# Score products of two pairs of heads in one visit, with the second pair in the banks that the products with V used

## The chip, the cores and the metric

The program runs on one core of one Trainium2 chip. Its time is the time of one execution on the device in microseconds; the runs before the change gave 1420.03, 1419.76 and 1416.32 us, median 1419.76 us. TensorE (PE in the profile) does the matrix products and writes them to PSUM, 8 banks of 512 float32 values in each of 128 partitions; VectorE (DVE), ScalarE (ACT) and GpSimd (POOL) do the rest, DVE and ACT alone reading PSUM here; SyncE (SP) issues nearly all DMAs.

## What is computed

The reference is an attention whose heads are mixed before and after the softmax, followed by two feed-forward blocks:

```python
scores = scale * np.matmul(q, k.transpose(0, 1, 3, 2))      # batch 4, heads 12, seq 448, dim 64
scores = np.einsum('bhij,hg->bgij', scores, w_pre)
attn = np.exp(scores - np.max(scores, axis=-1, keepdims=True))
attn = attn / (np.sum(attn, axis=-1, keepdims=True) + 1e-09)
attn = np.einsum('bhij,hg->bgij', attn, w_post)
x = np.matmul(attn, v)                                       # to (1792, 768)
h = x @ w_in;  x = (np.maximum(h, 0) ** 2) @ w_out           # 768 -> 2048 -> 768
h = x @ w_in2; x = (h * np.clip(h + 3, 0, 6) / 6) @ w_out2
```

## The kernel before

The four batches go in two groups of two. Each group is one attention stage and then one stage of both feed-forward blocks; the attention of the second group is opened (its first score chunk, its first tiles) behind the last units of the first group's feed-forward stage. On the trace the first attention stage ends at about 245 us, the second runs from about 722 to 947 us.

**The attention stage.** The 448 rows of a batch are cut into four chunks, c, of 110, 110, 110 and 118 rows, so a group has chunks 0 to 7. For each chunk the scores of the 12 heads are written to a tile `s(c)` in SBUF (two such tiles, in turn). A DMA then gathers tiles `t` of 10 rows by 12 heads, 120 partitions by 448 columns, 11 or 12 for a chunk and 90 for a group. The loop runs over these tiles, one in a slot i (`slot`, which follows the list `ORDER`). The steps look ahead: slot i fetches tile i+6 (`LOOK`), mixes tile i+3 with `w_pre` on PE (`premix`, tile `ps_m`, two PSUM banks in turn), takes its row maximum on DVE (`top`), the exponential of tile i+2 on ACT (`soft`, tile `p`), the reciprocal of the sums of tile i+1 on DVE (`guard`, `invert`), scales the mixing matrix with it on POOL (`scale`, tile `w2s`), and mixes tile i with it on PE (`postmix`, tile `ps_o`, two banks in turn); `keep` copies tile i-1 out of PSUM on DVE. `premix` and `postmix` are float32 products, which the trace shows as two matmuls for each one written.

**Work put into slots.** `plan` puts what belongs to other chunks into slots. The scores of a chunk, `score(c, k)`, go by pairs of heads k = 0 to 5. A pair lies in the two halves of the 128 partitions, so that its two matmuls work on 64 rows each and start together on PE; each pair takes three such products (high part with high part, low with high, high with low; fp32r). They are written to `bs`, one tile of two banks, of which there is one; a copy takes both banks to `s(c)`, on DVE for k = 2 and 5 and on ACT for the others. The list `when` has a slot for each k: for chunk c of 2 and over 0, 1, 3, 4 (or 5), 6 and 7 (or 8) slots after a start four slots ahead of chunk c-1; for chunk 1 of the second group the slots 0, 0, 1, 2, 3, 4. Chunk 1 of the first group uses unsplit float32 products (`score_first`) in slots 1, 2 and 3. In a slot, the scores stand on PE between `premix` and `postmix`.

The products with V of a finished chunk, `values(c, v)` for v = 0 and 1, are 24 written matmuls each, on 112 rows by 64 columns of the array; they stood in slot `f0 + 2`, f0 being the first slot of the next chunk, and wrote to `ps_x`, two banks in turn of the tag `bx`; DVE copies them to `xr`. V of the next batch is fetched one slot behind.

**The feed-forward stage.** Its units are `hidden` and `project`. `project` adds up in six accumulators, three output blocks d for each of the two batches e: d = 0 in the tag `bo`, d = 1 in the tag `bx`, d = 2 in the two banks of `bs`. In the last of eight units they are finished batch by batch (`finish`): for the first block by ACT (`yh`, L584) and DVE (`yl`, L585), for the second by a copy of ACT (L593). Within one engine everything runs in program order.

Of the kernel before, what the change touches and what calls it, by code (L numbers as in the profile page):

```python
# [7 lines left out]
F32 = mybir.dt.float32  # L8
# [3 lines left out]
AF = mybir.ActivationFunctionType  # L12
# [14 lines left out]
EARLY = 6  # L27
IDLE = 2
# [30 lines left out]
def attention_mlp_kernel(ctx: ExitStack, tc, qT, kT, v, w_pre, w_post, mask, w1_in, w1_out, w2_in, w2_out, outT):  # L59
    nc = tc.nc  # L60
    B, _, _, S = kT.shape
# [3 lines left out]
    P = 128  # L65
# [11 lines left out]
    DB = KC // DG  # L77
# [4 lines left out]
    ps = ctx.enter_context(tc.tile_pool(name="ps", bufs=2, space=PSUM))  # L82
    dr = ctx.enter_context(tc.tile_pool(name="dr", bufs=1, space=bass.MemoryType.DRAM))

    def bank(tag, name):
        return ps.tile([128, 512], F32, tag=tag, name=name)
# [12 lines left out]
    def load_constants():  # L99
        nc.sync.dma_start(out=mk, in_=mask)  # L100
        nc.sync.dma_start(out=wa, in_=w_pre)
        nc.sync.dma_start(out=wb, in_=w_post)
# [12 lines left out]
    class Attention:  # L115
# [60 lines left out]

        def score(self, c, k):
            n = CH[self.chunks[c][1]][1]
            if c < len(self.q_raw):
                for e in range(2):  # L180
                    self.score_first(bs[:n, e, :S], c, 2 * k + e)
            else:

                qh, ql = (x[:, k % (GB // 2), :n] for x in self.live["qq", c, 2 * k // GB])
                kh, kl = self.khl[:, 0, k, :], self.khl[:, 1, k, :]
                out = [bs[:n, e, :S] if self.ap else bank("bm", f"ps_s{self.gi}_{c}_{2 * k + e}")[:n, :S]
                       for e in range(2)]
                for m, (q, kk) in enumerate(((qh, kh), (ql, kh), (qh, kl))):
                    for e in range(2):
                        own = slice(e * D, (e + 1) * D)  # L190
                        nc.tensor.matmul(out[e], lhsT=q[own], rhs=kk[own], start=(m == 0), stop=(m == 2))  # L191
                if not self.ap:
                    for e in range(2):
                        nc.scalar.activation(self.s(c)[:n, 2 * k + e, :], out[e], AF.Copy)
            if self.ap and k % 3 == 2:
                nc.vector.tensor_copy(self.s(c)[:n, 2 * k:2 * k + 2, :], bs[:n, :, :S])
            elif self.ap:
                nc.scalar.activation(self.s(c)[:n, 2 * k:2 * k + 2, :], bs[:n, :, :S], AF.Copy)

        def s(self, c):  # L200
            if c not in self.ss:
# [83 lines left out]
        def values(self, c, v):  # L285
            b, ci = self.chunks[c]
            r0, n, _, _ = CH[ci]
            xo = bank("bx", f"ps_x{self.gi}_{c}_{v}")
            for k in range(PAIRS):
                for q in range(JC):  # L290
                    for e in range(2):
                        g = 2 * (v * PAIRS + k) + e
                        nc.tensor.matmul(  # L293
                            xo[e * D:(e + 1) * D, k * n:(k + 1) * n], lhsT=self.v[:, q, g, :],
                            rhs=self.aa[c][:, q, g, :n], start=(q == 0), stop=(q == JC - 1))
            if self.xr is None:
                self.xr = sh.tile([P, KC, T], F32, tag="xr", name=f"xr{self.gi}")
            c0 = (b % NB) * S + r0
            dst = self.xr[:, v * PAIRS:(v + 1) * PAIRS, c0:c0 + n]
            src = xo[:, :PAIRS * n].rearrange("p (k i) -> p k i", i=n)  # L300
            nc.vector.tensor_copy(dst, src)
# [7 lines left out]
        def first_opening(self):  # L309

            b, nk = self.batches[0], H // 2
            ns = [CH[ci][1] for ci in range(RAW)]
            raw = sh.tile([2 * D, nk * (S + sum(ns))], F32, tag="xr", name="first")
            self.k_raw = kr = raw[:, :nk * S].rearrange("p (k j) -> p k j", j=S)
            at = nk * S
            for n in ns:
                self.q_raw.append(raw[:, at:at + nk * n].rearrange("p (k r) -> p k r", r=n))
                at += nk * n
            idle = sh.tile([P, S], F32, tag="w0", name="idle", bufs=2)
            nc.gpsimd.memset(idle, 0.0)  # L320

            def load_q(c):
                r0, n = CH[c][:2]
                src = qT[b, :, r0 * nk:(r0 + n) * nk].rearrange("p (k r) -> p k r", k=nk)
                nc.sync.dma_start(out=self.q_raw[c], in_=src)

            for k in range(0, nk, 2):
                nc.sync.dma_start(out=kr[:, k:k + 2, :], in_=kT[b, k:k + 2].rearrange("k p j -> p k j"))
                if k == 0:
                    load_q(0)  # L330

            p = bank("bx", "ps_idle")
            for k in range(IDLE):
                nc.tensor.matmul(p[:, :S], lhsT=idle[:, :P], rhs=idle, start=(k == 0), stop=(k == IDLE - 1))
            load_constants()
            for c in range(1, RAW):
                load_q(c)
            for j in range(H + EARLY):
                c, h = j // H, j % H
                n = CH[c][1]  # L340
                p = bank(("bm", "bo")[j % 2], f"ps_s{self.gi}_{c}_{h}")
                self.score_first(p[:n, :S], c, h)
                if j % 2 == 0:
                    nc.scalar.activation(self.s(c)[:n, h, :], p[:n, :S], AF.Copy)
                else:
                    nc.vector.tensor_copy(self.s(c)[:n, h, :], p[:n, :S])
                if j == GB:
                    make_constants()
# [20 lines left out]
        def plan(self):  # L369

            def put(slot, fn, *args):
                self.at.setdefault(slot, []).append((fn, args))

            nch = len(self.chunks)
            for c in range(1, nch):
                f0, ns = self.first[c - 1], self.first[c] - self.first[c - 1]
                if c == 1:

                    at, when = f0, [f0 + k * 2 * (ns - LOOK) // H for k in range(H // 2)]
                else:  # L380

                    at = f0 - LOOK + 2
                    when = [at + k * 2 * (ns - 2) // H for k in range(H // 2)]
                if c < len(self.q_raw):
                    for k in range(EARLY // 2, H // 2):
                        put(k - EARLY // 2 + 1, self.score, c, k)
                    for k in range(H // 2):
                        put(4 + k * 3 // 2, self.part_first, k)
                    continue
                for k in range(H // GB):  # L390
                    put(when[k * GB // 2] - 5, self.fetch_q, c, k)
                    put(when[k * GB // 2] - 2, self.split_q, c, k)
                for k in range(H // 2):
                    put(when[k], self.score, c, k)
                b, ci = self.chunks[c]
                if ci == len(CH) - 1 and b != self.batches[-1]:
                    for k in range(H // 2):
                        put(at + 2 * k, self.fetch_k, b + 1, k)
                        put(at + 2 * k + 1, self.split_k, b + 1, k)
            for c in range(nch - 1):  # L400
                f0, ns = self.first[c + 1], self.first[c + 2] - self.first[c + 1]
                b, ci = self.chunks[c]
                for v in range(NV):
                    at = f0 + 2
                    put(at, self.values, c, v)
                    if ci == len(CH) - 1:
                        put(at + 1, self.fetch_v, b + 1, v)
            for v in range(NV):
                put(v, self.fetch_v, self.batches[0], v)
# [47 lines left out]
    class Mlps:  # L457
# [146 lines left out]
        def run(self, mp, behind):  # L604

            rest = None
            for n, (kind, which, m, _) in enumerate(self.units):
# [14 lines left out]
                if kind == "h":  # L622
                    if m == 0:
                        nm = f"{self.gi}_{which}"
                        self.gh, self.gl = {}, {}
                        gx = sh.tile([P, KC, T], F32R, tag="xr", name=f"gx{nm}")
                        for fc in range(NF):
                            for e in range(NB):
                                for part, of in (("h", self.gh), ("l", self.gl)):
# [4 lines left out]
                                    tag, bufs = SHARED.get((part, fc, e), (f"g{part}{fc}_{e}", 1))  # L634
# [11 lines left out]
                if u == 0:  # L646
                    acc = {}
                    for e in range(NB):
                        for d in range(DB):
                            nm = f"ps_a{self.gi}_{which}_{dg}_{d}_{e}"  # L650
                            if d < DB - 1:
                                acc[d, e] = bank(("bo", "bx")[d], nm)
                            else:
                                acc[d, e] = bank("bm", nm) if alone else bs[:, e, :]
                if m == 0 and which == 0:
# [10 lines left out]
                    behind[n - (len(self.units) - 1 - len(behind))]()  # L666

    bs = ps.tile([P, 2, 512], F32, tag="bs", name="bs", bufs=1)
    groups = B // NB
    with tc.manual_schedule():  # L670
        nc.vector.memset(half, 0.5)
# [70 lines left out]
```

## Time and profile before

| what | value |
| --- | --- |
| runs, median of 3 (lowest to highest) | 1419.76 us (1416.32 to 1420.03) |
| profiled execution, span from first to last instruction | 1417.4 us |
| PE busy | 1402.9 us (99%) |
| DVE, ACT, POOL busy | 669.0, 549.3, 384.7 us |
| bytes moved by DMA | 162.68 MB, mean 115 GB/s |
| lines of the chain that hold score products in `bs` and `ps_s` (L191) | 4%, under 1% |

For the profiled execution no time beside its span is given, so what lies around the span is not shown; the span lies within the three runs. A matmul's row gives its start well and its end by a model, so times on PE are best read from start to start. Idle time of an engine other than PE costs nothing by itself.

### The profile page before, as it was taken

Reading aid. Unit: us, or ns where it says so; the run is one execution under the profiler, and the core shown is the slowest. Engines: PE = TensorE matmul, PEld = TensorE weight load, DVE = VectorE, ACT = ScalarE, POOL = GpSimd, SP = SyncE. Lnnn points to the kernel's source line nnn. Section 1 sums busy time; section 2 is a strip of 40 time slices with the busy share of each in tenths; the row PEclk is TensorE's granted clock in tenths of the full one; section 3 lists DMA queues with packets and bytes.
Section 4 is the critical chain, followed back from the end, with each engine's and each line's share of the span. In section 5 each row is a group of like instructions: output and inputs, shape, how many; then the busy total and the mean of one; then the engine's idle time right before and its main releaser. Section 6 shows DMA issues by size and latency. Waiting matters only on the chain.

```text
span 1417.4 us, 22145 instructions
## 1 busy us (share of the span) xinstructions
PE 1402.9 (99%) x8500; PEld 1191.6 (84%) x8500; DVE 669.0 (47%) x1297; ACT 549.3 (39%) x1025; POOL 384.7 (27%) x431
## 2 busy tenths in 40 slices
PE   8999999999999999999999999999999999999998
PEld 4676778899989999988966677789999999999998
DVE  4776677877665688755536667751110102111000
ACT  3554344555332355534234534444341214443121
POOL 0222122433100133300012212145552223554221
PEclk9999999999999999999999999999999999999999
DMA  5453434555555455566544434321111111211121
GB/s 165 113 142 96 123 100 126 172 165 165 167 167 167 138 164 168 167 198 197 172 119 127 131 93 124 103 79 56 56 57 56 49 53 56 56 56 56 56 91 44
DMA packets 68367, 162.68 MB, mean 115 GB/s; under 512 B 6821, under 2 KB 43429, under 8 KB 68261
## 3 DMA queue, kind: packets, MB, share of 16 engines
q1 hardware_dynamic: 64805, 155.75, 37.5%
q10 hardware_dynamic: 3456, 5.51, 1.0%
q8 instruction: 67, 1.10, 0.3%
q14 instruction: 39, 0.32, 0.1%
HBM read 92.03 MB, written 30.67 MB: 87 GB/s over the span
## 4 chain that ended last, share of the span: by engine, by line
PE 96%; DVE 2%; DMA 1%; ACT 1%; issue 0%; SPq 0%; POOL 0%; DVEq 0%; ACTq 0%
PE ps_h L561 32%; PE ps_a L575 23%; PE ps_o L266 11%; PE ps_m L218 10%; PE bs L575 9%; PE ps_x L293 5%; PE bs L191 4%; DMA t<-s 1%; PE ps_s L306 1%; PE ps_s L191 0%; DMA first<-in_dram 0%; DVE arena L501 0%; DVE wl L519 0%; DVE yl L585 0%; DVE arena L504 0%
## 5 line engine op out<-in xcount | busy, mean ns | idle before, releaser
L266 PEld LDWEIGHTS ps_o<-w2s,p 120*112 120x112 f32 (+1 forms) x1440 | 168.3, 178 | 66.4 <-issue 40.8
L517 ACT ACTIVATE wh<-arena 128x768 fp32r<-128x768 f32 x128 | 107.4, 839 | 294.3 <-PE bs L575 247.2
L575 PE MATMUL ps_a<-gh,wh 128*128 128x448 f32 x544 | 199.7, 367 | 0.0
L575 PE MATMUL ps_a<-gh,wl 128*128 128x448 f32 x544 | 198.1, 364 | 0.0
L235 ACT ACTIVATE p<-ps_m,mx 120x448 f32<-120x448 f32 x180 | 113.9, 633 | 199.1 <-PE ps_o L266 149.3
L266 PE MATMUL ps_o<-w2s,p 120*112 120x120 f32 (+1 forms) x1440 | 186.0, 273 | 1.0 <-POOL w2s L255 1.0
L519 POOL TENSOR_TENSOR wl<-arena,wh 128x768 fp32r<-128x768 f32 x64 | 118.2, 1848 | 236.4 <-ACT wh L517 233.2
L218 PE MATMUL ps_m<-t,w1f 120*120 120x448 f32 x360 | 169.9, 555 | 3.7 <-DMA t<-s 3.7
L553 POOL TENSOR_TENSOR gl<-g,gh 128x448 fp32r<-128x448 f32 x80 | 98.7, 1234 | 227.1 <-ACT gh L552 179.0
L255 POOL TENSOR_SCALAR w2s<-w2f,rz 120x120 f32<-120x120 f32 x180 | 66.1, 367 | 346.4 <-DVE rz L247 315.5
L561 PE MATMUL ps_h<-xh,wh 128*128 128x448 f32 x384 | 140.6, 366 | 0.0
L561 PE MATMUL ps_h<-xh,wl 128*128 128x448 f32 x384 | 140.3, 365 | 0.1
L561 PE MATMUL ps_h<-yh,wh 128*128 128x448 f32 x384 | 140.3, 365 | 0.0
L561 PE MATMUL ps_h<-yh,wl 128*128 128x448 f32 x384 | 140.2, 365 | 0.0
L561 PE MATMUL ps_h<-xl,wh 128*128 128x448 f32 x384 | 139.6, 364 | 0.1
L561 PE MATMUL ps_h<-yl,wh 128*128 128x448 f32 x384 | 139.4, 363 | 0.0
L281 DVE COPY a<-ps_o 112x480 f32<-112x480 f32 (+1 forms) x176 | 114.8, 652 | 46.6 <-PE ps_o L266 38.2
L575 PE MATMUL ps_a<-gl,wh 128*128 128x448 f32 x340 | 124.7, 367 | 0.0
L227 DVE TENSOR_REDUCE mx<-ps_m 120x1 f32<-120x448 f32 x180 | 111.2, 618 | 22.5 <-PE ps_m L218 19.8
L519 DVE TENSOR_TENSOR wl<-arena,wh 128x768 fp32r<-128x768 f32 x64 | 62.7, 980 | 104.8 <-ACT wh L517 103.9
L575 PEld LDWEIGHTS ps_a<-gh,wh 128*128 128x128 f32 x544 | 102.1, 188 | 10.4 <-issue 2.5
L575 PEld LDWEIGHTS ps_a<-gh,wl 128*128 128x128 f32 x544 | 102.0, 188 | 9.4 <-issue 0.6
(83 smaller groups left out, 2264.1 us busy)
## 6 DMA issues: line engine op xcount, KB each, us to landing
arena<-in_dram SPq DMA_DIRECT2D x64, 768.0 KB
t<-s SPq DMA_DIRECT2D x176, 210.0 KB
keep<-arena SPq DMA_DIRECT2D x64, 384.0 KB
arena<-keep SPq DMA_DIRECT2D x64, 384.0 KB
v<-in_dram SPq DMA_DIRECT2D x8, 672.0 KB
outT_dram<-ot ACTq DMA_DIRECT2D x24, 224.0 KB
kr<-in_dram SPq DMA_DIRECT2D x18, 224.0 KB
qr<-in_dram SPq DMA_DIRECT2D x30, 110.0 KB
```

What stands on the lines that cost most here:

```text
L218: nc.tensor.matmul(m[:rows, :S], lhsT=w1f.rearrange("p i g -> p (i g)")[:rows, :rows], rhs=self.live.pop(("t", i))[:rows], start=True, sto ...
L227: nc.vector.reduce_max(mx[:rows], m[:rows, :S], axis=AX.X, negate=True)
L235: nc.scalar.activation(pt[:rows], m[:rows, :S], AF.Exp, bias=mx[:rows], accum_out=z[:rows])
L255: nc.gpsimd.tensor_scalar(w2s[:rows, :G * ni].rearrange("p (g i) -> p g i", g=G), w2f[:rows, :, :ni], rz[:rows], 1.0, op0=ALU.mult, op1=AL ...
L266: nc.tensor.matmul(o[:JP, q * G * ni:(q + 1) * G * ni], lhsT=pt[:rows, q * JP:(q + 1) * JP], rhs=w2s[:rows, :G * ni], start=True, stop=True)
L281: nc.vector.tensor_copy(dst, src)
L293: nc.tensor.matmul(xo[e * D:(e + 1) * D, k * n:(k + 1) * n], lhsT=self.v[:, q, g, :], rhs=self.aa[c][:, q, g, :n], start=(q == 0), stop=(q ...
L517: nc.scalar.activation(wh, self.wr(n), AF.Copy)
L519: eng.tensor_tensor(out=wl, in0=self.wr(n), in1=f(wh), op=ALU.subtract)
L553: nc.gpsimd.tensor_tensor(out=gl, in0=g, in1=f(gh), op=ALU.subtract)
L561: nc.tensor.matmul(hp[:, :S], lhsT=lw[:, c * P:(c + 1) * P], rhs=rw[:, c, cols], start=(k == 0), stop=(k == 3 * KC - 1))
L575: nc.tensor.matmul(acc[d, e][:, :S], lhsT=lw[:, wc], rhs=rw[fc, e], start=(fc == 0 and k == 0), stop=(fc == NF - 1 and k == 2))
```

## The change

Pairs with odd k are written to a second tile of two banks, `bx`, which now exists once, as `bs` does; the pair k+1 is put into the slot of pair k for even k, so two pairs follow each other in one visit of PE to the scores. `values` writes to the first bank of `bx` for v = 0 and to the second bank of `bs` for v = 1, and stands two slots later. In the feed-forward stage the block d = 1 adds up in the two banks of `bx`.

```diff
         def score(self, c, k):
             n = CH[self.chunks[c][1]][1]
+            two = (bs, bx)[k % 2]
             if c < len(self.q_raw):
                 for e in range(2):
-                    self.score_first(bs[:n, e, :S], c, 2 * k + e)
+                    self.score_first(two[:n, e, :S], c, 2 * k + e)
...
-                out = [bs[:n, e, :S] if self.ap else bank("bm", f"ps_s{self.gi}_{c}_{2 * k + e}")[:n, :S]
+                out = [two[:n, e, :S] if self.ap else bank("bm", f"ps_s{self.gi}_{c}_{2 * k + e}")[:n, :S]
...
             if self.ap and k % 3 == 2:
-                nc.vector.tensor_copy(self.s(c)[:n, 2 * k:2 * k + 2, :], bs[:n, :, :S])
+                nc.vector.tensor_copy(self.s(c)[:n, 2 * k:2 * k + 2, :], two[:n, :, :S])
             elif self.ap:
-                nc.scalar.activation(self.s(c)[:n, 2 * k:2 * k + 2, :], bs[:n, :, :S], AF.Copy)
+                nc.scalar.activation(self.s(c)[:n, 2 * k:2 * k + 2, :], two[:n, :, :S], AF.Copy)
...
         def values(self, c, v):
...
-            xo = bank("bx", f"ps_x{self.gi}_{c}_{v}")
+            xo = (bx, bs)[v % 2][:, v % 2, :]
...
                     for k in range(EARLY // 2, H // 2):
-                        put(k - EARLY // 2 + 1, self.score, c, k)
+                        put(1 if k == EARLY // 2 else 2, self.score, c, k)
...
                 for k in range(H // 2):
-                    put(when[k], self.score, c, k)
+                    put(when[k // 2 * 2], self.score, c, k)
...
                 for v in range(NV):
-                    at = f0 + 2
+                    at = f0 + 4
                     put(at, self.values, c, v)
...
-                            if d < DB - 1:
-                                acc[d, e] = bank(("bo", "bx")[d], nm)
+                            if d == 0:
+                                acc[d, e] = bank("bo", nm)
+                            elif d == 1:
+                                acc[d, e] = bx[:, e, :]
...
     bs = ps.tile([P, 2, 512], F32, tag="bs", name="bs", bufs=1)
+    bx = ps.tile([P, 2, 512], F32, tag="bx", name="bx", bufs=1)
```

PE in a steady stretch, first group, slots 18 to 20 (`ps_m` is a premix, `ps_o` a postmix, `qh`, `ql` and `khl` the parts of q and k). Before:

```order
L191 MATMUL bs<-khl_300,qh_3_0_670 118x448 x2
L191 MATMUL bs<-khl_300,ql_3_0_671 118x448 x2
L191 MATMUL bs<-khl_300,qh_3_0_670 118x448 x2
L266 MATMUL ps_o_18_719<-w2s_18_683,p_18_656 112x120 x4
L218 MATMUL ps_m_22_737<-t_22_648,w1f 120x448
L191 MATMUL bs<-khl_300,qh_3_0_670 118x448 x2
L191 MATMUL bs<-khl_300,ql_3_0_671 118x448 x2
L191 MATMUL bs<-khl_300,qh_3_0_670 118x448 x2
L266 MATMUL ps_o_19_748<-w2s_19_705,p_19_680 112x120 x4
```

And with the change:

```order
L192 MATMUL bs<-khl_300,qh_3_0_668 118x448 x2
L192 MATMUL bs<-khl_300,ql_3_0_669 118x448 x2
L192 MATMUL bs<-khl_300,qh_3_0_668 118x448 x2
L192 MATMUL bx<-khl_300,qh_3_0_668 118x448 x2
L192 MATMUL bx<-khl_300,ql_3_0_669 118x448 x2
L192 MATMUL bx<-khl_300,qh_3_0_668 118x448 x2
L267 MATMUL ps_o_18_724<-w2s_18_681,p_18_654 112x120 x4
L219 MATMUL ps_m_22_742<-t_22_646,w1f 120x448
L267 MATMUL ps_o_19_746<-w2s_19_703,p_19_678 112x120 x4
```

The second pair moved from slot 19 into the visit of slot 18, into `bx`. Over the whole program the visits to fp32r scores in slots are 77 before, one of them with two pairs, and 39 with the change, all with two; the pairs are 78 in both.

PE at the start of the second group's attention, slots 0 and 1. Before:

```order
L218 MATMUL ps_m_3_6697<-t_3_6499,w1f 120x448
L191 MATMUL bs<-khl_5895,qh_1_0_6563 110x448 x2
L191 MATMUL bs<-khl_5895,ql_1_0_6564 110x448 x2
L191 MATMUL bs<-khl_5895,qh_1_0_6563 110x448 x4
L191 MATMUL bs<-khl_5895,ql_1_0_6564 110x448 x2
L191 MATMUL bs<-khl_5895,qh_1_0_6563 110x448 x2
L266 MATMUL ps_o_0_6716<-w2s_0_6617,p_0_6556 112x120 x4
L218 MATMUL ps_m_4_6734<-t_4_6552,w1f 120x448
L191 MATMUL bs<-khl_5895,qh_1_1_6623 110x448 x2
```

And with the change:

```order
L219 MATMUL ps_m_3_6673<-t_3_6475,w1f 120x448
L192 MATMUL bs<-khl_5873,qh_1_0_6539 110x448 x2
L192 MATMUL bs<-khl_5873,ql_1_0_6540 110x448 x2
L192 MATMUL bs<-khl_5873,qh_1_0_6539 110x448 x2
L192 MATMUL bx<-khl_5873,qh_1_0_6539 110x448 x2
L192 MATMUL bx<-khl_5873,ql_1_0_6540 110x448 x2
L192 MATMUL bx<-khl_5873,qh_1_0_6539 110x448 x2
L267 MATMUL ps_o_0_6692<-w2s_0_6593,p_0_6532 112x120 x4
L219 MATMUL ps_m_4_6710<-t_4_6528,w1f 120x448
L192 MATMUL bs<-khl_5873,qh_1_1_6599 110x448 x2
```

Before, slot 0 already held two pairs, both written to `bs`; now the second of them goes to `bx`.

PE in the last unit of a `project`, second batch (e = 1), with what each row waits for in brackets (`gh`, `gx` are the inputs of the block, `wh`, `wl` the parts of the weights). Before:

```order
L575 MATMUL ps_a_0_0_0_1_3902<-gx_0_2854,wh_23_4183 128x448 [waits Pool_49]
L575 MATMUL ps_a_0_0_1_1_3903<-gh_0_14_1_2904,wh_23_4183 128x448
L575 MATMUL ps_a_0_0_1_1_3903<-gh_0_14_1_2904,wl_23_4184 128x448
L575 MATMUL ps_a_0_0_1_1_3903<-gx_0_2854,wh_23_4183 128x448
...
L575 MATMUL bs<-gh_0_14_1_2904,wh_23_4183 128x448 [waits DVE_49]
```

And with the change:

```order
L575 MATMUL ps_a_0_0_0_1_3885<-gx_0_2838,wh_23_4165 128x448 [waits Pool_49]
L575 MATMUL bx<-gh_0_14_1_2888,wh_23_4165 128x448 [waits DVE_49]
L575 MATMUL bx<-gh_0_14_1_2888,wl_23_4166 128x448
L575 MATMUL bx<-gx_0_2838,wh_23_4165 128x448
...
L575 MATMUL bs<-gh_0_14_1_2888,wh_23_4165 128x448 [waits DVE_49]
```

The order is the same, but the first matmul of block d = 1 has got a wait for DVE that only the one of `bs` had.

## Rows read from the trace of the kernel before

**Rows 1.** The page: span, and shares of the chain that ended last.

```profile
span 1417.4 us, 22145 instructions
...
PE 96%; DVE 2%; DMA 1%; ACT 1%; issue 0%; SPq 0%; POOL 0%; DVEq 0%; ACTq 0%
```

**Rows 2.** Timeline of PE, slots without scores: start us, us, instruction, count.

```profile
213.43 0.98 PE L266 MATMUL ps_o<-w2s,p 120*112 120x120 f32 x8
214.25 0.92 PE L218 MATMUL ps_m<-t,w1f 120*120 120x448 f32 x2
215.01 0.98 PE L266 MATMUL ps_o<-w2s,p 120*112 120x120 f32 x8
```

**Rows 3.** Timeline of PE, a slot with one score pair.

```profile
68.99 1.07 PE L266 MATMUL ps_o<-w2s,p 120*112 120x120 f32 x8
69.90 0.92 PE L218 MATMUL ps_m<-t,w1f 120*120 120x448 f32 x2
70.75 0.47 PE L191 MATMUL bs<-khl,qh 64*118 64x448 f32 x2
71.05 0.37 PE L191 MATMUL bs<-khl,ql 64*118 64x448 f32 x2
71.25 0.36 PE L191 MATMUL bs<-khl,qh 64*118 64x448 f32 x2
71.55 1.07 PE L266 MATMUL ps_o<-w2s,p 120*112 120x120 f32 x8
72.46 0.92 PE L218 MATMUL ps_m<-t,w1f 120*120 120x448 f32 x2
```

**Rows 4.** Score products by line 191: durations ns, first and last start us.

```profile
L191 PE MATMUL bs<-khl,qh x312: 355/449/462, 40.1 to 906.4; 64*110 64x448 f32 x108, 64*118 64x448 f32 x48
```

**Rows 5.** Timeline of ACT in that slot.

```profile
70.15 0.63 ACT L235 ACTIVATE p<-ps_m,mx 120x448 f32<-120x448 f32 x1
70.68 0.19 ACT L235 ACTIVATION_READ_ACCUMULATOR p<-ps_m,mx 120x1 f32 x1
71.66 0.92 ACT L198 ACTIVATE s<-bs 118x896 f32<-118x896 f32 x1 [0.78 <-PE bs L191]
```

**Rows 6.** Timeline of PE at the start of the second group's attention.

```profile
721.97 0.92 PE L218 MATMUL ps_m<-t,w1f 120*120 120x448 f32 x2
722.92 0.46 PE L191 MATMUL bs<-khl,qh 64*110 64x448 f32 x2
...
725.27 0.46 PE L191 MATMUL bs<-khl,qh 64*110 64x448 f32 x2 [1.49 <-ACT s L198]
...
726.15 1.94 PE L266 MATMUL ps_o<-w2s,p 120*112 120x120 f32 x8
...
731.15 0.92 PE L218 MATMUL ps_m<-t,w1f 120*120 120x448 f32 x2
```

**Rows 7.** Windows there: us, busy by engine, granted clock, DMA share, GB/s.

```profile
721.00:725.90 4.90, 3.38 (x20) 1.95 (x18) 1.52 (x5) 2.02 (x4) 0.37 (x1) 1.00 1.01 344
725.90:729.30 3.40, 3.40 (x14) 2.06 (x10) 0.73 (x2) 1.92 (x4) 0.25 (x1) 0.50 0.55 155
```

**Rows 8.** Timeline, PE and DVE at the end of a projection.

```profile
417.85 0.36 PE L575 MATMUL ps_a<-gh,wh 128*128 128x448 f32 x1
...
418.02 1.15 DVE L585 TENSOR_TENSOR yl<-ps_a,yh 128x448 fp32r<-128x448 f32 x2
...
418.87 0.37 PE L575 MATMUL ps_a<-gx,wh 128*128 128x448 f32 x1
419.09 0.61 DVE L585 TENSOR_TENSOR yl<-bs,yh 128x448 fp32r<-128x448 f32 x1
...
419.75 0.47 PE L575 MATMUL bs<-gh,wh 128*128 128x448 f32 x1 [0.52 <-DVE yl L585]
```

**Rows 9.** Waits of PE: total us, times, longest us.

```profile
PE bs L575 <- DVE yl L585: 1.0, 2, 0.5
```

**Rows 10.** Timeline of PE, first group, slot 5.

```profile
36.00 0.98 PE L218 MATMUL ps_m<-t,w1f 120*120 120x448 f32 x2 [0.26 <-DMA t<-s]
```

**Rows 11.** Timeline of PE, products with V in a slot without scores.

```profile
219.73 0.98 PE L266 MATMUL ps_o<-w2s,p 120*112 120x120 f32 x8
220.64 4.74 PE L293 MATMUL ps_x<-a,v 112*64 112x110 f32 x96
225.31 1.01 PE L218 MATMUL ps_m<-t,w1f 120*120 120x448 f32 x2
226.16 0.98 PE L266 MATMUL ps_o<-w2s,p 120*112 120x120 f32 x8
```

More of the change, by code (lines that the diff above doesn't have):

```diff
@@ L330, in first_opening @@
                     load_q(0)
-            p = bank("bx", "ps_idle")
             for k in range(IDLE):
-                nc.tensor.matmul(p[:, :S], lhsT=idle[:, :P], rhs=idle, start=(k == 0), stop=(k == IDLE - 1))
+                nc.tensor.matmul(bx[:, 0, :S], lhsT=idle[:, :P], rhs=idle, start=(k == 0), stop=(k == IDLE - 1))
             load_constants()
```

## The prediction

> **What bounds the kernel now.** I read the page first: PE makes up 96% of the chain that ended last over a span of 1417.4 us [rows 1]. So only three things can change the time: what PE works, how long it waits, and its clock. A PE that is always busy can still lose time between matmuls, so the second view is the timeline of PE, read from start to start. A slot without scores lasts 215.01 - 213.43 = 1.58 us, 0.82 from postmix to premix and 0.76 back [rows 2]. A slot with one pair lasts 71.55 - 68.99 = 2.56 us [rows 3], 0.98 more. The reader is to see where the 0.98 lies. Between the second and third product of the pair there are 0.20 us (71.05 to 71.25), between the first and second 0.30, and from the third to the postmix 0.30; the premix ahead takes 0.85 to the next start in place of 0.76, and the postmix behind 0.91 in place of 0.82. So three products at 0.20 are 0.61 us, and 0.37 us is lost around them, about 0.09 on either side of the change to products of 64 rows and on either side of the change back. No row there shows PE waiting for another engine; it is a price per visit, not per pair. The third view is the waits of PE, for where that does not hold.
>
> **The change part by part.** Steady visits. One line shows 312 matmuls of `bs<-khl,qh` [rows 4], four for a pair, so 78 pairs; they stand in 77 visits before and 39 with the change. Each of the 38 visits that go gives back 0.37 us, if the second pair's products follow at 0.20 us: 38 x 0.37 = 14.1 us. The rows show no second pair right behind a first one without a wait, so this term has two ends. The upper is the 0.37. At the lower, the second pair pays the 0.10 us again that stands between first and second product, and as much at its own entry, and gives back 0.18: 6.8 us. I take the upper: the pairs differ in bank and weights alone, and second and third product also differ in weights and stand at 0.20.
>
> The Trainium skill (TensorEngine Tiling (Array Packing), Key Properties) says that changing the tiling mode, not just the tile, drains TensorE. The trace agrees, with 0.09 us ahead of either change of shape [rows 2, 3], but it also shows 0.09 behind either, which the page does not name. By the page alone only the two drains, 0.18 us a visit, would go, which is the lower end; by the rows all four go.
>
> Second pair in `bx`. What hides the copies: in a visit at T, ACT copies `bs` from T + 0.90 (70.75 to 71.66) for 0.92 us, `bx` then to about T + 2.75, and the exponential queued behind them takes 0.63 [rows 5], so it frees its PSUM bank at T + 3.4. PE wants that bank for the premix two slots on, at T + 1.40 (two pairs) + 0.91 + 0.76 + 0.82 = T + 3.89. Cover 0.5 us, cost 0. For k = 2 and 5 one copy is on DVE, which makes it wider. The copies read other banks than PE writes, and the next visit is three slots away.
>
> Start of the second group. There slot 0 already has two pairs, both in `bs`, and the second waited 1.49 us for ACT's copy of the first (725.27) [rows 6]. From 725.9 to 729.3 the granted clock was 0.50, the 1.2 GHz level, and 1.00 on both sides; the fall came behind that wait [rows 7]. From premix to premix of the next-but-one slot it took 731.15 - 721.97 = 9.18 us [rows 6]. The parts of the steady rows give 0.85 + 1.40 + 0.91 + 0.85 + 0.80 + 0.91 = 5.72 for the same products, so 3.46 us are lost. Now the second pair goes to `bx`, which is free (it holds a block finished ahead of the one in `bs`). The first still waits for `bs`, 0.1 us. Gain 3.4 us, half of it the wait and half (3.40 x 0.50 = 1.7) the clock. What is late next: pair k = 2 in slot 1 needs `bs` copied by ACT, which now can start as before at about 724.3 and ends at 725.2, and PE comes there at about 726. Ends: 3.4, or 1.7 if the clock still falls.
>
> Feed-forward. Block d = 1 moves into one tile of two banks and gets a wait for DVE in the second batch. What such a wait does, `bs` shows: its matmul started at 419.75, where the one ahead (418.87) and 0.20 us made 419.07 due, and right after DVE had read the *other* bank of the same tile (419.09 + 0.61 = 419.70) [rows 8]. So a read of either half holds back a write to the other. For d = 1 the read ends at 418.02 + 1.15 = 419.17 and PE wants the bank at 417.85: 1.37 us late in place of 0.68, and `bs` then comes at 420.5, after its reads. Price 0.69 us each. The waits of PE have two of these [rows 9], both in the first group's first block, where DVE also prepares weights: 1.4 us together. In the other six endings PE never waited at `bs`, and by the spacing of 1.22 us between blocks it won't at `bx`. Ends: 0 to 3 us.
>
> The Trainium skill (PSUM, "PSUM bank collisions raise a hardware error") reports that TensorE writing one bank while VectorE reads another runs clean. By that the wait would not be needed, and without it the sum would be 1.4 us better; the row shows that the program makes PE wait all the same.
>
> At nothing: the products with V two slots later. They pay for their own two changes of shape in a slot without scores (0.91 ahead of them and 0.85 behind, for 0.82 and 0.76 [rows 2, 11]), no less and no more beside scores. In their new place the banks have been free for a slot, and the next visit comes three slots later. The copies to `xr` stay on DVE. The one merged visit of the first group's chunk 1: PE then waits for a fetched tile in slot 5 anyway (0.26 us in the row, and the postmix ahead was over before) [rows 10], so 0.4 us earlier there becomes waiting. Gathers of `s` start no later than before, since the last pair of a chunk now stands up to two slots earlier; SP's queue keeps its order but for the fetch of V, which moves with the products.
>
> The sum: -14.1 - 3.4 + 1.4 = -16.1 us. Against the profiled execution's span of 1417.4 this is 1401.3; what lies around the span is not given. The median of the runs is 1419.8, 2.4 above the span, so for a median I take 1403.7.
>
> **The rivals.**
> - *The second pair pays too.* As above, 6.8 in place of 14.1 us: 1411.0. For it: the 0.10 us between first and second product is there in every visit, and no row has two pairs back to back. Against: nothing changes in shape between the pairs. Chance 0.13.
> - *The clock still falls at the second group's start.* For it: it fell there once; DMA was at a share of 1.01 then, so something else may come late. Against: the only wait of PE ahead of the fall goes. 1403.7 + 1.7 = 1405.4. Chance 0.16.
> - *ACT becomes the bound (slower).* Two copies of 0.92 us stand ahead of an exponential that frees the premix's bank. If another ACT job, the split of q or of k, falls in between, the cover of 0.5 us is gone, and each us more stops PE in each of the 39 visits. It decides from 16.1 / 39 = 0.41 us of waiting a visit on; a whole further copy is 39 x 0.92 = 35.9 us: 1439.6. Against: in the 1.58 us of a plain slot ACT has 0.82 to do [rows 5], and two plain slots follow each visit. Chance 0.04.
> - *The gathers become the bound, and the gain turns into waiting (no change).* For it: slot 5 of the first group waits for one. Against: the plain slots at 1.58 us each [rows 2] are the fastest there are, and PE does not wait in them; they do not get faster. 1418 to 1420. Chance 0.04.
> - *Better than forecast*: the added waits at `bx` don't show, and early waits shrink: 1400. Chance 0.05.
>
> **How the numbers follow.** The forecast, 1401.5 to 1405 for itself, has 0.58. The range from 1399 to 1411 takes in the second and third case and the better one and leaves out the last stretch of the first rival, the slower one and no change, about 0.15. A difference under 0.3% (4.3 us) can't be told from none. Faster is the forecast, the clock, the second pair and the better case, 0.92; the same 0.04; slower 0.04.
>
> **What would show it.** Right: in the changed profile visits of 12 score matmuls, with the fourth product 0.20 us behind the third; a slot with a visit lasting 1.58 + 0.37 + 6 x 0.20 = 3.17 us, not 3.35; the wait of 1.49 us and the granted clock of 0.50 gone at the second group's start; two waits of PE of about 1.2 us for `yl` at `bx` and none at `bs`. Wrong: a wait of PE for ACT's copy or exponential in the slot behind a visit, fresh waits for gathered tiles, or a clock of 0.50 in either attention stage past its start.

## The result and the profile after

| what | before | after |
| --- | --- | --- |
| runs, median (lowest to highest), 4 each | 1418.85 us (1416.32 to 1420.03) | 1405.28 us (1403.79 to 1408.13) |
| span of the profiled execution | 1417.4 us | 1401.9 us |

The changed kernel takes 0.9909 of the time before (95% interval 0.9897 to 0.9921): it is faster by 12.9 us (11.2 to 14.6). Its profiled execution took 1403.79 us as the runs are timed, so 1.9 us lie around the span. The forecast was 1403.7 us.

The page after, span and the chain's shares (it answers to [rows 1]):

```profile
span 1401.9 us, 22130 instructions
...
PE 95%; DVE 2%; ACT 1%; DMA 1%; issue 1%; POOL 0%; SPq 0%; ACTq 0%; POOLq 0%; DVEq 0%
```

PE makes up 95% of the chain, nearly as before: such a share tells nothing of a gain that lies between products of an engine that counts as busy there. The timeline of PE in a slot with a visit shows it (start us, us, instruction; compare [rows 3]):

```profile
65.26 0.92 PE L219 MATMUL ps_m<-t,w1f 120*120 120x448 f32 x2
66.11 0.47 PE L192 MATMUL bs<-khl,qh 64*118 64x448 f32 x2
66.41 0.36 PE L192 MATMUL bs<-khl,ql 64*118 64x448 f32 x2
66.61 0.36 PE L192 MATMUL bs<-khl,qh 64*118 64x448 f32 x2
66.81 0.36 PE L192 MATMUL bx<-khl,qh 64*118 64x448 f32 x2
...
67.22 0.36 PE L192 MATMUL bx<-khl,qh 64*118 64x448 f32 x2
67.52 1.07 PE L267 MATMUL ps_o<-w2s,p 120*112 120x120 f32 x8
68.43 0.92 PE L219 MATMUL ps_m<-t,w1f 120*120 120x448 f32 x2
```

The fourth product, the first into `bx`, stands 0.20 us behind the third (66.61 to 66.81), as the third behind the second. The larger steps are at the change of shape alone: 0.85 ahead (65.26 to 66.11), 0.30 behind the first product and behind the last, 0.91 behind the postmix. From premix to premix it is 68.43 - 65.26 = 3.17 us.

The start of the second group, PE (compare [rows 6]):

```profile
716.54 0.92 PE L219 MATMUL ps_m<-t,w1f 120*120 120x448 f32 x2
717.49 0.45 PE L192 MATMUL bs<-khl,qh 64*110 64x448 f32 x2
718.19 0.37 PE L192 MATMUL bx<-khl,qh 64*110 64x448 f32 x2
718.89 1.07 PE L267 MATMUL ps_o<-w2s,p 120*112 120x120 f32 x8
...
722.96 0.54 PE L219 MATMUL ps_m<-t,w1f 120*120 120x448 f32 x1
```

And windows there (us; busy and count of PE, PEld, DVE, ACT, POOL; granted clock; DMA share; GB/s; compare [rows 7]):

```profile
716.50:723.00 6.50, 6.47 (x46) 4.17 (x46) 4.03 (x10) 3.79 (x8) 0.73 (x2) 1.00 0.86 280
723.00:730.00 7.00, 7.00 (x46) 4.74 (x45) 5.74 (x14) 3.82 (x10) 1.75 (x4) 1.00 0.15 36
```

The second pair follows the first without a wait, and the granted clock stays at 1.00, the level of 2.4 GHz. From premix to the next premix but one there are now 722.96 - 716.54 = 6.42 us in place of 9.18, with one pair's products (0.61) more in between.

The waits of PE (total us, times, longest; compare [rows 9]):

```profile
PE bx L575 <- DVE yl L585: 2.4, 2, 1.2
PE ps_o L267 <- POOL w2s L256: 1.8, 5, 0.5
```

The two waits at `bx` in the feed-forward are there, and none at `bs` is left. New are three waits for `w2s`, the scaled mixing matrix, of 0.26 us each (2 waits before, 5 now), which the prediction had not named. The list also puts two waits of a premix for its tile, 0.92 us at 31.08 and 1.38 at 34.27, down to ACT. They are no sign of late copies: the exponentials that free the two banks had ended at 29.31 and 30.88, and the kernel before waits there too, for gathered tiles (1.2 to 1.9 us a time in e7 and e8). Past the first 40 us PE waits for no gathered tile in any of these runs.

The time by stage, for four profiled executions. Each stretch is the distance of two matmul starts on PE; "start" is from the span's begin to premix 10. Since that first stretch differs from execution to execution (37.5 to 41.5 us in the five profiles with its visit merged, 39.0 to 40.0 in the five without), what the change does is read from the others.

| stretch, us | before | before, e8 | after | e3 |
| --- | --- | --- | --- | --- |
| start, to premix 10 | 39.22 | 40.03 | 37.48 | 38.29 |
| rest of the first attention | 205.02 | 205.03 | 199.95 | 198.29 |
| first feed-forward, to premix 93 | 477.73 | 477.75 | 479.11 | 479.12 |
| second group's start, premix 93 to 95 | 9.18 | 7.32 | 6.42 | 6.42 |
| rest of the second attention | 215.63 | 215.51 | 208.32 | 207.50 |
| second feed-forward, to the end | 470.65 | 470.64 | 470.63 | 470.63 |

Without the start, before and after differ by -5.07 + 1.38 - 2.76 - 7.31 - 0.02 = -13.8 us; with e8 as the kernel before it is -11.8. The start adds -1.7 to the difference of the two spans, -15.5; since starts with the merged visit lie on both sides of those without, that part is taken as chance.

### The profile page after: what moved, and what is told of

Same layout as the page of the kernel before. It is cut to its first block, busy times and chain, and to the rows that moved or that the text cites. A ratio compares the mean times of both kernels' runs of the same rounds, so it can differ in the third digit from the quotient of the medians.

```text
span 1401.9 us, 22130 instructions
## 1 busy us (share of the span) xinstructions
PE 1385.5 (99%) x8500; PEld 1194.9 (85%) x8500; DVE 670.8 (48%) x1297; ACT 549.3 (39%) x1025; POOL 385.5 (27%) x431
## 4 chain that ended last, share of the span: by engine, by line
PE 95%; DVE 2%; ACT 1%; DMA 1%; issue 1%; POOL 0%; SPq 0%; ACTq 0%; POOLq 0%; DVEq 0%
PE ps_h L561 33%; PE ps_a L575 12%; PE bx L575 11%; PE ps_o L267 11%; PE bs L575 10%; PE ps_m L219 9%; PE bx L294 3%; PE bs L294 2%; PE bs L192 2%; PE bx L192 2%; DMA t<-s 0%; PE ps_s L307 0%; PE ps_s L192 0%; DVE arena L501 0%; DMA first<-in_dram 0%
## 5 line engine op out<-in xcount | busy, mean ns | idle before, releaser
L267 PE MATMUL ps_o<-w2s,p 120*112 120x120 f32 (+1 forms) x1440 | 181.2, 269 | 2.0 <-POOL w2s L256 1.8
L575 PE MATMUL ps_a<-gh,wh 128*128 128x448 f32 x288 | 106.5, 370 | 0.0
L575 PE MATMUL ps_a<-gh,wl 128*128 128x448 f32 x288 | 104.8, 364 | 0.0
L542 DVE SCALAR_TENSOR_TENSOR g<-r,ps_h 128x448 f32<-128x448 f32 x64 | 39.7, 620 | 119.0 <-ACT r L541 115.9
L575 PE MATMUL bx<-gh,wh 128*128 128x448 f32 x256 | 93.4, 365 | 2.4 <-DVE yl L585 2.4
L575 PE MATMUL bx<-gh,wl 128*128 128x448 f32 x256 | 93.3, 364 | 0.0
```

Source lines behind the costliest of these rows:

```text
L267: nc.tensor.matmul(o[:JP, q * G * ni:(q + 1) * G * ni], lhsT=pt[:rows, q * JP:(q + 1) * JP], rhs=w2s[:rows, :G * ni], start=True, stop=True)
L575: nc.tensor.matmul(acc[d, e][:, :S], lhsT=lw[:, wc], rhs=rw[fc, e], start=(fc == 0 and k == 0), stop=(fc == NF - 1 and k == 2))
```

## The experiments

The theory was that of the prediction: a price per change of shape, the bank that makes the second pair possible, a wait and the clock at the second group's start, and two new waits in the feed-forward. The rivals: that the new place of the products with V carries some of the gain, that the second bank alone does, and that ACT's two copies cost something after all. Each edit is against the changed kernel but for e2 (against the kernel before). Times are medians, ratios against runs of the kernel before on the same chip.

**e1: one pair a visit again.** All the rest of the change stays.

```diff
-                        put(1 if k == EARLY // 2 else 2, self.score, c, k)
+                        put(k - EARLY // 2 + 1, self.score, c, k)
...
-                    put(when[k // 2 * 2], self.score, c, k)
+                    put(when[k], self.score, c, k)
```

> The changed kernel with one pair of heads in a visit again, as before the change, and all else as changed (odd pairs in bx, products with V two slots later, block d = 1 in bx). My theory (a visit has a price of 0.37 us for its two changes of shape): 38 visits come back, of which 36 to 38 cost 0.37 us, and the small waits for ACT behind double visits go, about 2.5 us; so 11 to 12 us over the changed kernel's 1405.3, about 1417, and 2 us under the kernel before, because the second group's start keeps its gain of 3.4 us and the feed-forward stage its loss of 1.4. Rival (the gain comes from the second tile, which frees PE of waits, and not from the number of visits): within 2 us of the changed kernel. In the trace a slot with one pair lasts 2.56 us, the wait of 1.49 us at the second group's start stays away and the clock there stays at 1.00.

Measured: 1417.39 us (11 runs), 0.9992 of before (0.9983 to 1.0001), 12.1 us over the changed kernel. Its stretches were 205.19, 479.16, 5.81 and 215.70: both attention stages as before, the second group's start without the wait, the feed-forward with its 1.4 us. So the merged visits carry the gain, and what else the change does nearly cancels.

**e2: two pairs a visit, both in `bs`.** The order of the change without its bank.

```diff
-                    put(when[k], self.score, c, k)
+                    put(when[k // 2 * 2], self.score, c, k)
```

> The kernel before with two pairs in a visit, both in the one tile bs, and nothing else changed. My theory: the second pair waits in every visit for ACT's or DVE's copy of the first, about 1.5 to 1.7 us from the end of the first pair, in 39 visits; less the 14 us for fewer visits the kernel is some 45 us slower than before, about 1463. Rival (the copy is quick enough beside other work of PE, and the number of visits is all that counts): 14 us faster than before, 1405.

Measured: 1457.45 us (2 runs), 1.0275 of before (1.0257 to 1.0294), 39 us slower. The third and the fourth product of a visit, on PE:

```profile
111.84 0.36 PE L191 MATMUL bs<-khl,qh 64*110 64x448 f32 x2
...
113.39 0.46 PE L191 MATMUL bs<-khl,qh 64*110 64x448 f32 x2 [1.19 <-DVE z L241]
```

And its waits of PE:

```profile
PE bs L191 <- ACT s L198: 27.1, 26, 1.9
...
PE bs L191 <- DVE z L241: 11.9, 10, 1.2
PE bs L191 <- DVE s L196: 3.7, 3, 1.3
```

All 39 visits wait for the first pair's copy, 42.7 us together; in the ten that are put down to `z` DVE had copied the pair just before (here from 112.25 to 113.34). 36 of the visits take 2.66 to 2.87 us in place of 1.40, the other three 2.90 to 3.55. That is 1.26 to 1.47 more for most, where 1.5 to 1.7 were expected, so the loss is 39 us and not 45. So merging gains only with the second bank; without it the gain turns into a loss of three times its size.

**e3: the copy of each pair in `bx` on DVE.** Then ACT never copies two in a row.

```diff
-            if self.ap and k % 3 == 2:
+            if self.ap and k % 2 == 1:
```

> The changed kernel with the copies of odd k (from bx) on DVE and those of even k (from bs) on ACT, so that no visit puts two copies on ACT. My theory (the seven waits of PE of 0.3 to 0.5 us, 2.5 us together, in the slots behind a double visit come from ACT's queue of two copies and a split of k ahead of the exponential): these waits go, 2 to 2.5 us under the changed kernel, 1403. Rival (DVE, which mixes, copies and reduces in each slot, becomes late instead): waits of PE for DVE's row maximum or for w2s in as many slots, and the time the same or up to 5 us more.

Measured: 1403.6 us (4 runs), 0.9897 of before (0.9883 to 0.9910). The intervals of e3 and of the changed kernel overlap; the stages settle it. The first attention went from 199.95 to 198.29, the second from 208.32 to 207.50, 2.5 us together, and the waits for `w2s` are 2 again, of 1.0 us, as before. This place shows how. The changed kernel, timelines of all engines:

```profile
93.02 0.64 ACT L236 ACTIVATE p<-ps_m,mx 120x448 f32<-120x448 f32 x1 [1.02 <-DVE z L242]
...
93.41 0.46 PE L192 MATMUL bs<-khl,qh 64*110 64x448 f32 x2
...
94.30 0.92 ACT L199 ACTIVATE s<-bs 110x896 f32<-110x896 f32 x1 [0.56 <-PE bs L192]
...
95.12 0.91 ACT L199 ACTIVATE s<-bx 110x896 f32<-110x896 f32 x1
...
95.92 0.58 ACT L150 ACTIVATE khl<-kr 128x448 fp32r<-128x448 f32 x1
...
96.38 0.64 ACT L236 ACTIVATE p<-ps_m,mx 120x448 f32<-120x448 f32 x1
...
96.53 0.63 DVE L151 TENSOR_TENSOR khl<-kr,khl 128x448 fp32r<-128x448 f32 x1 [2.39 <-ACT khl L150]
...
97.07 0.15 DVE L242 TENSOR_SCALAR z<-z 120x1 f32<-120x1 f32 x1
97.13 0.65 DVE L282 COPY a<-ps_o 112x480 f32<-112x480 f32 x1
...
97.29 0.92 PE L219 MATMUL ps_m<-t,w1f 120*120 120x448 f32 x2
97.70 0.15 DVE L248 RECIPROCAL rz<-z 120x1 f32<-120x1 f32 x1
...
98.04 0.37 POOL L256 TENSOR_SCALAR w2s<-w2f,rz 120x120 f32<-120x120 f32 x1 [3.88 <-DVE rz L248]
...
98.46 1.07 PE L267 MATMUL ps_o<-w2s,p 120*112 120x120 f32 x8 [0.26 <-POOL w2s L256]
```

The same place in e3, which is 0.35 us ahead:

```profile
94.77 0.57 ACT L150 ACTIVATE khl<-kr 128x448 fp32r<-128x448 f32 x1
...
95.58 0.61 DVE L151 TENSOR_TENSOR khl<-kr,khl 128x448 fp32r<-128x448 f32 x1
...
96.94 0.92 PE L219 MATMUL ps_m<-t,w1f 120*120 120x448 f32 x2
97.08 0.36 POOL L256 TENSOR_SCALAR w2s<-w2f,rz 120x120 f32<-120x120 f32 x1 [3.28 <-DVE rz L248]
...
97.69 0.98 PE L267 MATMUL ps_o<-w2s,p 120*112 120x120 f32 x8
```

A part of k is split by two engines: ACT makes the high part (L150) and DVE, from it, the low part (L151). In the changed kernel ACT's half stands behind the two copies and ends at 95.92 + 0.58 = 96.50. DVE's half waits 2.39 us for it and starts at 96.53. DVE works in program order, so the three steps ahead of `w2s` stand behind it: the guard of the sum (`z`, 97.07), a copy of 0.65 us and the reciprocal (97.70). `w2s` is done at 98.04 + 0.37 = 98.41, and the postmix comes 98.46 - 97.29 = 1.17 us behind the premix. The sum had long been there: counted in order, the `z` at 97.07, the `w2s` at 98.04 and the exponential at 93.02 belong to one tile, since the steps look ahead. In e3 ACT's half starts one copy sooner (94.77), DVE's half at 95.58 without a wait, `w2s` is done at 97.08 + 0.36 = 97.44, and the postmix comes 0.75 us behind the premix (96.94 to 97.69). So the expected cause, ACT's queue of copies and a split, is there, but the way to PE does not lead through the exponential behind them (96.38), as the expectation had it; it leads through DVE's half of the split.

There are six such places (seven were expected), with a premix at 42.23, 49.05, 76.33, 97.29, 770.42 and 791.38; in each of them DVE waits 0.8 to 2.4 us for ACT's half, and in e3 in none. In three of them two copies stand ahead of ACT's half (the postmix is 0.42 late), in three a copy of `bx` (0.22 or 0.23); the premix behind each comes 0.09 later too: 1.93 + 0.55 = 2.5 us. The wait list names only three waits of 0.26 us for all this, so the sum is from starts.

**e4: another order of finishing.** At the end of the first feed-forward block, for the first batch, DVE reads block 0 last. (The edit holds for both groups; only the first had the wait.)

```diff
-                        self.finish(which, dg, e, range(DB), acc)
+                        self.finish(which, dg, e, (1, 2, 0) if e == 0 and which == 0 else range(DB), acc)
```

> The changed kernel with the blocks of the first batch finished in the order d = 1, 2, 0 in the first feed-forward block, so that DVE reads bx first. My theory: the two waits of PE at bx, 1.2 us each in the trace, fall to about 0.7 us, as the read of bx ends one DVE step of 0.53 us sooner; 1.0 to 1.1 us under the changed kernel, which the trace shows and the times hardly. Rival (the wait is for DVE's weight preparation, or for the other bank's reads in whatever order): the waits stay at 1.2 us.

Measured: 1404.66 us (4 runs), 0.9902 of before (0.9889 to 0.9916), which as a time can't be told from the changed kernel. Its wait of PE:

```profile
PE bx L575 <- DVE yl L585: 1.4, 2, 0.7
```

The wait fell from 2.4 to 1.4 us, with nothing but the order of the reads changed.

**e5: the products with V in their old slot.**

```diff
-                    at = f0 + 4
+                    at = f0 + 2
```

> The changed kernel with the products with V two slots after the next chunk's first, as before the change, so in the same slot as the last visit to the scores. My theory (the later place is there because the banks are shared now: the first product with V has to wait until DVE has copied the pair k = 5 out of bx): from the end of that pair to the end of DVE's copy it takes about 1.2 us, of which the postmix between them covers 0.9; a wait of PE of about 0.3 us ahead of each of 12 to 14 pairs of products, 4 us over the changed kernel, 1409. Rival (the two slots cost and give nothing at all): the same as the changed kernel, 1405, and no wait of PE for DVE at L294.

Measured: 1410.13 us (4 runs), 0.9940 of before (0.9922 to 0.9958); by the ratios 0.0031 x 1418 = 4.4 us over the changed kernel. One of its twelve meetings, on PE and DVE:

```profile
82.69 1.07 PE L267 MATMUL ps_o<-w2s,p 120*112 120x120 f32 x8
82.80 1.09 DVE L197 COPY s<-bx 118x896 f32<-118x896 f32 x1 [0.19 <-PE bx L192]
...
83.94 1.26 PE L294 MATMUL bx<-a,v 112*64 112x110 f32 x22 [0.18 <-DVE s L197]
```

The products with V come right behind a visit and wait for DVE to empty `bx`: 83.94 - 82.69 = 1.25 us behind the postmix, for 0.91 in [rows 11]. The stages give 1.9 and 1.6 us more, and twelve waits at 1.25 - 0.91 = 0.34 us make 4.1. So no gain is left that the later slot would earn beside the wait that it avoids; it pays for the bank that the pairs have taken.

**e6: e3 and e4 together.**

> The changed kernel with the copies of odd k on DVE and with the blocks of the first batch finished in the order 1, 2, 0 in the first feed-forward block, both edits tried alone already (1403.6 and 1404.7 us against 1405.3). If they are independent, as they lie in different stages, 2.5 + 1.0 us under the changed kernel: 1402, ratio 0.988 to the kernel before. If one gives back the other, no better than 1403.6.

Measured: 1401.92 us (4 runs, 1401.22 to 1404.22), 0.9883 of before (0.9868 to 0.9899), the lowest median here, with an interval that still overlaps those of e3 and of the changed kernel. Its stretches: 198.29, 478.10, 6.41, 207.52. Against the changed kernel that is -1.66 - 1.01 - 0.01 - 0.80 = -3.5 us.

**e7 and e8: the kernel before, profiled twice more.** No edit.

> The kernel before once more, for its clock at the second group's start. If the wait of 1.49 us there brings the clock to 0.50 each time, the row of 0.50 after about 726 us is there again and 3.4 us are lost there; if the fall depends on more than the wait (in the kernel with both pairs in one tile PE waited 1.90 us there and the clock stayed at 1.00), the clock can stay at 1.00, and then the stretch from premix to premix takes 7.5 us in place of 9.2.

> The same look again, on the same grounds: 0.50 after about 726 us and 9.2 us from premix to premix if the wait alone decides, or 1.00 and 7.5 us in some executions if it does not.

Measured: 1418.97 and 1418.06 us. The second group's start took 9.25 us in e7 and 7.32 in e8. The window behind the wait in e7:

```profile
725.34:728.70 3.36, 3.36 (x15) 2.58 (x16) 0.21 (x1) 1.13 (x2) 0.00 (x0) 0.50 0.60 177
```

Of e8:

```profile
726.00:730.00 4.00, 4.00 (x29) 2.64 (x30) 1.96 (x4) 1.92 (x4) 0.98 (x2) 1.00 0.62 184
```

And PE in e8, the same wait as in [rows 6]:

```profile
725.88 0.45 PE L191 MATMUL bs<-khl,qh 64*110 64x448 f32 x2 [1.26 <-ACT s L198]
```

The wait is there each time (1.49 us in the first profile, 1.60 in e7, 1.26 in e8); the fall of the clock behind it is in two of three, those with the longer waits.

## Why the prediction was right, and where it was not

*Steady visits, -14.1: held.* In e3, where no split comes late, the first attention is 205.02 - 198.29 = 6.73 us shorter: 18 visits at 0.374. The second is 8.0 to 8.1 shorter (before at 215.51 to 215.63), of which 0.61 are the products of the pair that now stands ahead of premix 95; 7.4 to 7.5 over 20 visits are 0.37 each. All four sides of the two changes of shape count, the upper end, and *the second pair pays too* falls with the 0.20 us between third and fourth product.

The Trainium skill (TensorEngine Tiling (Array Packing), Key Properties) speaks of a drain at a change of the mode. By the two drains alone, 0.18 us a visit, the gain would have been 6.8 us; the runs give 14.1, so the time behind each change must be counted as well.

*Second pair in `bx`, cost 0: this step failed,* by 2.5 us. The prediction followed one job behind ACT's copies, the exponential, to the bank that it frees, and that part held: the premix at 97.29 stands 97.29 - 93.41 = 3.88 us behind the visit's start, as forecast (T + 3.89), and its bank was free at 96.38 + 0.64 = 97.02, even with a split of k ahead of the exponential. What it did not follow is the split itself. DVE's half of it waits for ACT's half, and behind DVE's half stands the way to `w2s` and the postmix; that cost was put at nothing. It falls due only where a split stands in the slot of a visit, six times. In a visit without one, at 122.43, both copies are on ACT as well, and `w2s` is done at 125.87 + 0.37 = 126.24, 0.84 us ahead of its postmix at 127.08. The prediction had named a split between copies and exponential, but in a rival, as time on the exponential's way and in each of 39 visits; ACT did not become the bound.

*Start of the second group, -3.4: half of it holds each time.* With the same products between the two premixes, e1 takes 5.81 us; the profiles of before 9.18, 9.25 and 7.32. So it gains 3.4 us where the clock would have fallen and 1.5 where not. Both ends of the term were right; to take one of them from a single profile as the value was not. The rival that the clock still falls in the changed kernel is not what was seen: it stayed at 1.00 there. What failed is that the kernel before doesn't always lose those 1.9 us (9.18 or 9.25 against 7.32).

*Feed-forward, +1.4: held.* The stage is 479.11 - 477.73 = 1.38 us longer. The place that answers to [rows 8], in the changed kernel:

```profile
410.81 0.37 PE L575 MATMUL ps_a<-gx,wh 128*128 128x448 f32 x1
...
411.73 0.61 DVE L585 TENSOR_TENSOR yl<-bx,yh 128x448 fp32r<-128x448 f32 x1
...
412.40 0.47 PE L575 MATMUL bx<-gh,wh 128*128 128x448 f32 x1 [1.22 <-DVE yl L585]
```

The product into `bx` starts 412.40 - 410.81 = 1.59 us behind the one ahead, 1.39 more than the usual 0.20, when DVE's read of `bx` has ended (411.73 + 0.61 = 412.34); the forecast was 1.37. e4 moves that read and the wait moves with it.

*Products with V, first merged visit, gathers, at nothing:* nothing in the stages or in the waits speaks against them. e5 shows what the two slots are for. That the first visit's gain is lost in waiting was not tried by itself.

*The sum.* -16.1 was forecast; the stages give -13.8 without the start, and the runs -12.9 (-11.2 to -14.6). The 2.5 us of the late splits are the difference of the first two within 0.2. The rest may be executions of the kernel before that keep their clock; if that is one of three, as in the profiles, it makes 1.9 / 3 = 0.6 us, an estimate. That the predicted span (1401.3) and the profiled one (1401.9) nearly agree is in part the luck of a start that was 1.7 us shorter. The forecast difference is 3.2 us too large and lies outside the measured interval. The forecast median is nearer, 1.6 us under the measured one and inside the range, in part by luck too: it was counted from a median of 1419.8 us, which the fourth run of the kernel before lowered to 1418.85.

## What to carry to other kernels

Where PE changes between products of two array shapes, read the price from start to start on both sides of each change, and gather the products of one shape into fewer visits; but only with a bank for each, since in one bank PE waits for the copy between them. For each engine that then gets its jobs in a row, count all other jobs that can fall into that slot, and follow each job that is queued behind them to PE, also where the way leads through another engine: a job there that waits holds up what stands behind it, though that has nothing to do with the copies. A term read from one execution, above all one that holds a clock, deserves a second profile before it enters the sum in full.

## What was not expected of the hardware

The price of the visit is not seen with split products alone: in the start of the changed kernel, float32 products of 64 rows show the same pattern on PE.

```profile
24.98 0.92 PE L219 MATMUL ps_m<-t,w1f 120*120 120x448 f32 x2
25.82 1.01 PE L307 MATMUL bs<-first 64*110 64x448 f32 x4
...
27.51 1.07 PE L267 MATMUL ps_o<-w2s,p 120*112 120x120 f32 x8
28.42 0.92 PE L219 MATMUL ps_m<-t,w1f 120*120 120x448 f32 x2
```

The first of them stands 0.84 us behind the premix, for 0.76 without scores, and the premix 0.91 behind the postmix, for 0.82 [rows 2]. That it is the change of shape that costs is argued from such rows; no run here tried other shapes.

A wait of PE does not settle whether the clock falls. Behind 1.49 us, and 1.60 us in e7, the granted clock went to 0.50, the level of 1.2 GHz; behind 1.26 us in e8 it stayed at 1.00. By these three the longer wait decides, but in e2 it stayed at 1.00 too, though PE waited 1.90 us at the same place and about 1 us in most visits (PE, then windows, of e2):

```profile
744.82 0.46 PE L191 MATMUL bs<-khl,qh 64*110 64x448 f32 x2 [1.90 <-ACT s L198]
```

```profile
746.00:752.00 6.00, 4.76 (x32) 2.93 (x31) 3.11 (x7) 2.98 (x7) 0.70 (x2) 1.00 0.24 63
```

What decides stays open. So does what makes the start differ by up to 4 us: over 20 to 30 us the mean granted clock was 0.69 in the first profile of the kernel before and 1.00 in that of the changed one, but 1.00 also in e7 and e8, whose starts took 38.96 and 40.03 us.
